# Keys of three units loaded as 32x32 blocks: VectorE's transposes behind the last item of a unit, stores on ScalarE's queue

## The chip, the cores and the metric

The kernel runs on one core of one Trainium2 chip. Times are device microseconds (us) of whole executions; a profile shows one execution. The engines are named as in the profile: PE is TensorE (matrix products), PEld its weight loads, DVE is VectorE, ACT ScalarE, POOL GpSimd, SP SyncE, which here only issues transfers; "ACTq" and "SPq" are transfers issued by ACT and SP. Every run told here was in the fast state.

## The reference, cut to what matters

A retention block (a causal linear attention with a decay per head) feeds a multiplicative feed-forward network, all in float32.

```python
# q, k, v: (8 batches, 8 heads, 576 positions, 64)
scores = q @ k.T / 8
ret    = scores * gamma[h] ** (i - j)   # for i >= j, else 0
x      = (ret @ v)  as (8*576, 512)
a, b   = x @ w1, x @ w2                 # (512, 1024) each
out    = ((a * b) @ w3) @ w_out         # (1024, 1024), (1024, 512)
```

## The kernel before

The attention works in *units*: a pair of batches (four pairs) and one of five chunks of positions (one of 64 and four of 128), so units 0 to 19. A unit needs q and k transposed (`qT`, `kT`), scores `sc`, their product with the mask `pm`, the output products `xps`, and a running state `st`. Between the units stand *items* of the feed-forward part: `up` (seven products, 9.1 us of PE) and `down` (seven products, 12.1 us of PE, followed by stores of 128 rows twice). From the second pair on, the feed-forward part of one pair fills the gaps of the next pair's attention.

The transposes come in two kinds. `front` transposes on PE and copies from PSUM with ScalarE. `front_blocks` needs an operand that was loaded as 32x32 blocks, placed so that VectorE's transposes within the blocks give the whole transpose; such a load is 16 small transfers of 32 KB for a unit of 128 positions.

```python
def load_blocks(g, nm):                       # 16 issues for 128 positions
    t = pools["ld"].tile([P, 2 * NP, P // BL, BL], F32, tag="ld_q", name="bl_" + nm)   # two buffers
    for a in range(2):
        for f in range(D // BL):
            for m in range(n):
                nc.sync.dma_start(t[part:part + BL, :, m, :], ...)
def front_blocks(g, names="kq"):
    for nm in names:
        dst = pools["fr"].tile(..., tag=nm + "T", bufs=1 if nm == "k" else 2)
        nc.vector.transpose(dst[...], live["bl_" + nm, g][...])
# ... cut ...
in_blocks = [u > 2 * NC for u in range(G)] + [False] * 2     # NC = 5: k by blocks from unit 11 on
for g in range(NC, G):
    n = -(-len(todo) // (NC - c))                            # items of this unit
    if g + 2 < G and not in_blocks[g + 2]:
        load(g + 2, "k"); load_blocks(g + 2, "q")
    if g + 1 < G:
        scale(g + 1, "v")                                    # GpSimd
        if not in_blocks[g + 1]:
            front(g + 1, "k")                                # PE transposes
            front_blocks(g + 1, "q")                         # VectorE transposes
    half = (n + 1) // 2
    if in_blocks[g + 1]:
        scale_blocks(g + 1)                                  # GpSimd scales q's blocks
        work(1)
        front_blocks(g + 1)
        half = max(half - 1, 0)
    if in_blocks[g + 2]:
        load_blocks(g + 2, "q"); load_blocks(g + 2, "k")
    work(half)
    pv(g)                                                    # output products
    # ... loads of v (and k) of unit g + 2, then:
    state(g + 1); score(g + 1)
    work(n // 2)
```

`aside` is a list of VectorE operations; each addition inside an `up` item takes one from it, and a `down` item empties it before its last addition. In `down` the output buffer `ot` exists once, so its first copy must wait for the stores of the item before.

Of the kernel before, what the change touches and what calls it, by code (L numbers as in the profile page):

```python
# [40 lines left out]
def kernel(  # L41
# [13 lines left out]
    nc = tc.nc  # L55
# [13 lines left out]
    NC = (S + P - 1) // P  # L69
# [3 lines left out]
    G = NB2 * NC  # L73
    NB = 3
# [5 lines left out]
    NQ = DF // QC  # L80
# [26 lines left out]
    def load(g, names, engine=nc.sync):  # L107
        i, c = divmod(g, NC)
        sz = sizes[c]
        src = {"k": k, "q": q, "v": v}  # L110
        for nm in names:
            t = pools["ld"].tile([P, 2 * H, D], F32, tag="ld_" + nm, name="ld_" + nm)
            engine.dma_start(
                t[:sz], src[nm][2 * i:2 * i + 2, :, starts[c]:starts[c] + sz, :].rearrange("b h p d -> p (b h) d"))
            live[nm, g] = t
# [27 lines left out]
    for c in (0, slice(1, NC)):  # L143
        n = short if c == 0 else P
# [34 lines left out]
    def load_blocks(g, nm):  # L179

        i, c = divmod(g, NC)
        n = sizes[c] // BL
        t = pools["ld"].tile([P, 2 * NP, P // BL, BL], F32, tag="ld_q", name="bl_" + nm)
        src = {"k": k, "q": q}[nm][2 * i:2 * i + 2].rearrange("b (p a) s d -> a (b p) s d", a=2)
        for a in range(2):
            for f in range(D // BL):
                part = (a * (D // BL) + f) * BL
                for m in range(n):
                    s0 = starts[c] + m * BL
                    nc.sync.dma_start(t[part:part + BL, :, m, :],  # L190
                                      src[a, :, s0:s0 + BL, f * BL:(f + 1) * BL].rearrange("m r x -> r m x"))
        live["bl_" + nm, g] = t

    def scale_blocks(g):
        c = g % NC
        n, n0 = sizes[c] // BL, starts[c] // BL
        t = live["bl_q", g]
        for b in range(2):
            part = t[:, b * NP:(b + 1) * NP, :n, :]
            nc.gpsimd.tensor_tensor(  # L200
                out=part, in0=part, in1=gqs[:, :, n0:n0 + n].unsqueeze(3).to_broadcast([P, NP, n, BL]),
                op=ALU.mult)

    def front_blocks(g, names="kq"):
        c = g % NC
        n = sizes[c] // BL
        for nm in names:
            dst = pools["fr"].tile([P, 2, NP, P], F32, tag=nm + "T", name=nm + "T", bufs=1 if nm == "k" else 2)
            nc.vector.transpose(
                dst[:, :, :, :sizes[c]].rearrange("p b m (n x) -> p (b m) n x", x=BL),  # L210
                live["bl_" + nm, g][:, :, :n, :])
            live[nm + "T", g] = dst

    def scale(g, nm, scalar=False):
        c = g % NC
        sz = sizes[c]
        t, gam = live[nm, g], {"q": gq, "v": gk}[nm]
        t = t[:sz].rearrange("p (b h) d -> p b h d", b=2)
        if scalar:
            for h in range(H):  # L220
                nc.scalar.mul(t[:, :, h, :], t[:, :, h, :], gam[:sz, c, h:h + 1])
            return
        nc.gpsimd.tensor_tensor(  # L223
            out=t, in0=t, in1=gam[:sz, c].unsqueeze(1).unsqueeze(3).to_broadcast([sz, 2, H, D]), op=ALU.mult)

    def front(g, names="kq"):
        c = g % NC
        sz = sizes[c]
        for nm in names:
            src = live[nm, g]  # L230
            dst = pools["fr"].tile([P, 2, NP, P], F32, tag=nm + "T", name=nm + "T",
                                   bufs=1 if nm == "k" and g >= NC else 2)
            for b in range(2):
                tp = acc.tile([P, NP, P], F32, tag="acc", name="tp")
                for p in range(NP):
                    h = b * H + 2 * p
                    nc.tensor.transpose(tp[:, p, :sz],  # L237
                                        src[:sz, h:h + 2, :].rearrange("p a d -> p (a d)"),
                                        ident[:sz, :sz])
                nc.scalar.copy(dst[:, b, :, :sz], tp[:, :, :sz])  # L240
            live[nm + "T", g] = dst

    def score(g):
        c = g % NC
        sz = sizes[c]
        kT, qT = live["kT", g], live["qT", g]
        pm = pools["fr"].tile([P, 2, 2, NP, P], F32, tag="pm", name="pm", bufs=1)
        for b in range(2):
            sc = [acc.tile([P, NP, P], F32, tag="acc", name="sc") for j in range(2)]
            for p in range(NP):  # L250
                for j, hs in enumerate(heads):
                    nc.tensor.matmul(sc[j][:sz, p, :sz], kT[hs, b, p, :sz], qT[hs, b, p, :sz],  # L252
                                     start=True, stop=True)
            for j in range(2):
                nc.vector.tensor_mul(pm[:sz, b, j, :, :sz], sc[j][:sz, :, :sz],  # L255
                                     mask[:sz, :sz].unsqueeze(1).to_broadcast([sz, NP, sz]))
        live["pm", g] = pm
# [284 lines left out]
    aside = []  # L542
# [53 lines left out]
    def ahead(x, y, n=3):  # L596
        todo_sums = pair_of(x, y)[2]
        for _ in range(min(n, len(todo_sums))):
            aside.append(todo_sums.pop(0))
# [60 lines left out]
    stores, keep_stores = [], []  # L660

    def store():
        while stores:
            nc.sync.dma_start(*stores.pop(0))


    load_block()
# [85 lines left out]
    todo = [(0, 1, 2), (0, 0, 3), (0, 1, 3)] + [(0, 2, fp) for fp in range(NQ - 1)]  # L753
# [34 lines left out]
    todo = [(down, (0, 0), (0, 1)), (down, (1, 0), (1, 1)), (down, (0, 2), (1, 2))]  # L788

    def add_pair(i):  # L790

        for n in range(NB):
            m = every.index((i, n))
            if m != NB:
                todo.append((up, i, n, 1))
            if m > NB and m % 2 == 0:
                todo.append((down, (m - 2, 2), (m - 1, 2)))
            todo.extend((up, i, n, fp) for fp in range(2, NQ))
            if m + 1 < len(every):
                todo.append((up, *every[m + 1], 0))  # L800
                if m % 2 == 0:
                    todo.append((carry, m, 2))
            else:
                todo.append((down, (m - 1, 2), (m, 2)))
            todo.append((down, (m, 0), (m, 1)))

    def work(n):
        for _ in range(min(n, len(todo))):
            fn, *args = todo.pop(0)

            nxt = next((x for x in todo if x[0] is not carry), None)
            if nxt and nxt[0] is down and fn is not carry:
                if fn is down:
                    args.append(nxt[1:])
                else:
                    last = args == [*every[max(nxt[1][0], nxt[2][0])], NQ - 1]
                    ahead(*nxt[1:], 1 if last else 3)
            if g == G and not todo:
                fn(*args, last=True)
            else:  # L820
                fn(*args)

    g = NC
# [3 lines left out]
    state(NC)  # L827
    score(NC)
    scale_blocks(NC + 1)
    in_blocks = [u > 2 * NC for u in range(G)] + [False] * 2  # L830
    for g in range(NC, G):
        c = g % NC
        n = -(-len(todo) // (NC - c))
        if g + 2 < G and not in_blocks[g + 2]:
            load(g + 2, "k")
            load_blocks(g + 2, "q")
        if g + 1 < G:
            scale(g + 1, "v")
            if not in_blocks[g + 1]:
                front(g + 1, "k")  # L840
                front_blocks(g + 1, "q")
        half = (n + 1) // 2
        if in_blocks[g + 1]:
            scale_blocks(g + 1)
            work(1)
            front_blocks(g + 1)
            half = max(half - 1, 0)
        if in_blocks[g + 2]:
            load_blocks(g + 2, "q")
            load_blocks(g + 2, "k")  # L850
        work(half)
        pv(g)

        if g + 2 < G:
            queue = nc.scalar if in_blocks[g + 2] else nc.sync
            load(g + 2, "v", queue)
            if in_blocks[g + 2] and (g + 2) % NC != NC - 1:
                load(g + 2, "k", queue)
        if g + 1 < G:
            state(g + 1)  # L860
            score(g + 1)
        if g + 2 < G and not in_blocks[g + 2]:
            scale_blocks(g + 2)
        if g == NC + 1:
            strassen_tokens(1, 0)
            todo.extend((up, 1, 0, fp) for fp in range(2))
        work(n // 2)
        if c == NC - 1:
            add_pair(g // NC)
    g = G  # L870
# [44 lines left out]
```

## Time and profile before

| | before |
|---|---|
| median of three runs | 863.84 us (861.37 to 864.35) |
| span of the profiled run | 858.3 us |
| PE busy | 846.7 us |
| VectorE, ScalarE, GpSimd busy | 475.0, 182.2, 115.9 us |
| PE idle between 225 and 840 us | 0.22 us |

A busy PE is read together with its waits. An engine that is busy all the time and waits for nothing sets the time by the sum of its instructions. The prediction below shows the lines.

### The profile page before, as it was taken

What the parts mean: (1) busy time and instruction counts of PE and PEld (TensorE: products, weight loads), DVE (VectorE), ACT (ScalarE), POOL (GpSimd) and SP (SyncE); (2) the same over time, 40 slices, a digit from 0 to 9 for tenths busy, and PEclk for the clock granted to TensorE, in tenths of its full rate; (3) what the DMA queues carried; (4) which work ended last, traced back from release to release, by engine and by line L of the source; (5) the groups of instructions that cost most, each with busy time, mean ns of one, the idle gap of its engine ahead of it and who ended that gap; (6) DMA issues with size and microseconds to landing.
All of it is one profiled execution on the core that took longest, in us unless ns stands there. A gap on an engine that the chain in (4) does not pass through costs nothing.

```text
span 858.3 us, 15385 instructions
## 1 busy us (share of the span) xinstructions
PE 846.7 (99%) x6317; PEld 773.3 (90%) x6317; DVE 475.0 (55%) x794; ACT 182.2 (21%) x364; POOL 115.9 (14%) x96
## 2 busy tenths in 40 slices
PE   9999999999999999999999999999999999999998
PEld 8889999544998999999999999999999999999996
DVE  4899998995754344553544443535543334335343
ACT  3766333342122111101101101111101101001000
POOL 3000020001214214203023120230400101000000
PEclk9999999999999999999999999999999999999999
DMA  9994453455247524415231525061200000000001
GB/s 197 228 213 115 100 100 99 123 147 81 33 105 142 97 49 83 80 42 107 53 70 28 89 45 115 19 106 25 51 25 26 2 25 1 26 25 1 25 1 49
DMA packets 205062, 63.21 MB, mean 74 GB/s; under 512 B 186936, under 2 KB 195384, under 8 KB 204992
## 3 DMA queue, kind: packets, MB, share of 16 engines
q1 hardware_dynamic: 172352, 54.07, 30.5%
q10 hardware_dynamic: 32640, 8.16, 5.0%
q8 instruction: 49, 0.80, 0.4%
q14 instruction: 21, 0.17, 0.1%
HBM read 52.76 MB, written 9.44 MB: 72 GB/s over the span
## 4 chain that ended last, share of the span: by engine, by line
PE 88%; DVE 3%; SPq 1%; issue 1%; DMA 1%; ACT 0%; DVEq 0%; ACTq 0%
PE up L506 46%; PE po L617 25%; PE ps L461 6%; PE sc L252 4%; PE xps L309 3%; PE xps L302 2%; PE st L274 1%; PE tp L237 1%; SPq L746 1%; DVE c L511 1%; DMA raw<-in_moe_w_out_dram 0%; DVE e L400 0%; SPq L349 0%; DVE w L411 0%; DMA out_dram<-ot 0%
## 5 line engine op out<-in xcount | busy, mean ns | idle before, releaser
L511 DVE TENSOR_TENSOR c<-up,c 128x384 f32<-128x384 f32 x240 | 133.2, 555 | 183.8 <-PE up L506 179.1
L506 PE MATMUL up<-xT,wA 128*128 128x192 f32 x1152 | 212.0, 327 | 0.6 <-ACT c L519 0.6
L506 PEld LDWEIGHTS up<-xT,wA 128*128 128x128 f32 x1152 | 190.6, 190 | 3.1 <-ACT c L519 0.9
L506 PE MATMUL up<-T,wS 128*128 128x192 f32 x768 | 140.5, 326 | 0.0
L506 PEld LDWEIGHTS up<-T,wS 128*128 128x128 f32 x768 | 127.4, 190 | 0.0
L617 PE MATMUL po<-w3o,ab 128*128 128x256 f32 x456 | 104.2, 380 | 0.3 <-ACT ot L639 0.3
L617 PEld LDWEIGHTS po<-w3o,ab 128*128 128x128 f32 x456 | 85.9, 190 | 12.3 <-ACT ot L639 0.7
L621 DVE TENSOR_TENSOR ot<-po,ot 128x256 f32<-128x256 f32 x90 | 38.2, 424 | 74.4 <-PE po L617 71.6
L506 PE MATMUL up<-xT,wS 128*128 128x192 f32 x384 | 70.6, 327 | 0.6 <-DVE c L511 0.5
L531 ACT COPY c<-up 128x384 f32<-128x384 f32 x48 | 22.9, 478 | 225.5 <-PE up L506 221.3
L255 DVE TENSOR_TENSOR pm<-sc,mask 128x512 f32<-128x512 f32 (+1 forms) x80 | 45.5, 629 | 45.1 <-PE sc L252 45.1
L506 PE MATMUL up<-T,wA 128*128 128x192 f32 x384 | 70.3, 326 | 0.0
L617 PE MATMUL po<-wB,forms 128*128 128x256 f32 x288 | 65.3, 379 | 0.0
L506 PEld LDWEIGHTS up<-xT,wS 128*128 128x128 f32 x384 | 63.5, 190 | 1.5 <-DVE c L511 1.5
L506 PEld LDWEIGHTS up<-T,wA 128*128 128x128 f32 x384 | 63.7, 190 | 0.0
L617 PEld LDWEIGHTS po<-wB,forms 128*128 128x128 f32 x288 | 54.6, 190 | 7.7 <-issue 0.3
L223 POOL TENSOR_TENSOR ld_v<-ld_v,gk 128x1024 f32<-128x1024 f32 (+1 forms) x17 | 32.8, 1928 | 198.7 <-DMA ld_v<-in_v_dram 160.7
L461 PE MATMUL ps<-wo,w3T 128*128 128x512 f32 x128 | 55.4, 593 | 1.3 <-DVE w3T L415 1.3
L461 PEld LDWEIGHTS ps<-wo,w3T 128*128 128x128 f32 x128 | 23.9, 190 | 32.1 <-issue 30.5
L480 POOL TENSOR_TENSOR T<-xT,T 128x384 f32<-128x384 f32 x20 | 20.9, 1044 | 214.0 <-PE up L506 212.4
L537 DVE TENSOR_TENSOR ab<-c 128x768 f32<-128x768 f32 x48 | 47.0, 980 | 3.8
L519 ACT COPY c<-up 128x384 f32<-128x384 f32 x48 | 22.9, 477 | 118.8 <-PE up L506 70.1
(77 smaller groups left out, 817.2 us busy)
## 6 DMA issues: line engine op xcount, KB each, us to landing
raw<-in_moe_w_dram SPq DMA_DIRECT2D x64, 128.0 KB, 3.0
bl_q<-in_q_dram SPq DMA_DIRECT2D x208, 32.0 KB, 2.2
out_dram<-ot SPq DMA_DIRECT2D x23, 256.0 KB, 2.0
bl_k<-in_k_dram SPq DMA_DIRECT2D x136, 32.0 KB, 2.3
raw<-in_moe_w_dram SPq DMA_DIRECT2D x8, 512.0 KB, 7.5
raw<-in_moe_w_dram SPq DMA_DIRECT2D x16, 256.0 KB, 6.7
ld_k<-in_k_dram SPq DMA_DIRECT2D x8, 512.0 KB, 7.8
ld_v<-in_v_dram SPq DMA_DIRECT2D x8, 512.0 KB, 7.4
```

What stands on the lines that cost most here:

```text
L223: nc.gpsimd.tensor_tensor(out=t, in0=t, in1=gam[:sz, c].unsqueeze(1).unsqueeze(3).to_broadcast([sz, 2, H, D]), op=ALU.mult)
L252: nc.tensor.matmul(sc[j][:sz, p, :sz], kT[hs, b, p, :sz], qT[hs, b, p, :sz], start=True, stop=True)
L255: nc.vector.tensor_mul(pm[:sz, b, j, :, :sz], sc[j][:sz, :, :sz], mask[:sz, :sz].unsqueeze(1).to_broadcast([sz, NP, sz]))
L309: nc.tensor.matmul(banks[r][heads[half], b, n, :sz], vs[:sz, b * H + 2 * p + j, :], pm[:sz, b, j, p, :sz], start=(c == 0 and m == 0), stop ...
L461: nc.tensor.matmul(ps, live["w3T", ft][:, g, :], live["wo"][:, g, :], start=(g == 0), stop=(g == KF - 1))
L506: nc.tensor.matmul(ps[:, w, :], a[:, w, r, :], b[:, r, :], start=(new and w == r == 0), stop=(w == r == 1), skip_group_check=True)
L511: nc.vector.tensor_add(c[:, to], ps, c[:, sb])
L519: nc.scalar.copy(c[:, 0], p1)
L531: nc.scalar.copy(c[:, 0], p1)
L537: nc.vector.tensor_mul(ab[:, 4 * fp:4 * fp + 4, :], c[:, :, 0, :], c[:, :, 1, :])
L617: nc.tensor.matmul(ps[nm], a[A][:, f, :], live["W"][B][:, f, :], start=(f == 0 and not on), stop=(f == NP - 1), skip_group_check=True)
L621: nc.vector.tensor_add(ot[:, to[0], to[1]], ps[nm], ot[:, sb[0], sb[1]])
```

## The change

Its intent is to take PE's transposes of k out of three more units: 8 and 9 (the second pair's last two) and 10 (the third pair's short one). To make room, items move between units 7 to 9, VectorE's transposes go behind all items of a unit, and stores go out on ScalarE's queue. Cut to its core:

```diff
     def store():
         while stores:
-            nc.sync.dma_start(*stores.pop(0))
+            nc.scalar.dma_start(*stores.pop(0))
...
-            todo.extend((up, i, n, fp) for fp in range(2, NQ))
+            if m != NB:
+                todo.extend((up, i, n, fp) for fp in range(2, NQ))
...
-    in_blocks = [u > 2 * NC for u in range(G)] + [False] * 2
+    in_blocks = [u >= 2 * NC - 2 for u in range(G)] + [False] * 2
...
-        n = -(-len(todo) // (NC - c))
+        n = (1, 1, 1, 3, 1)[c] if g < 2 * NC else -(-len(todo) // (NC - c))
...
             scale_blocks(g + 1)
+            work(n - 1)
+            aside.extend(lambda nm=nm: front_blocks(g + 1, nm) for nm in "kq")
             work(1)
-            front_blocks(g + 1)
-            half = max(half - 1, 0)
+            while aside:
+                aside.pop(0)()
+            half = 0
...
-            todo.extend((up, 1, 0, fp) for fp in range(2))
-        work(n // 2)
+            todo.extend((up, 1, 0, fp) for fp in range(NQ))
+        if not (in_blocks[g + 1] and g + 1 < G):
+            work(n // 2)
```

## The prediction

> **What bounds the kernel now.** I read the page's busy shares first, then the stretches by window, the waits of TensorE, and the chain of waits in order of time around the units that the change touches.
>
> ```profile
> span 858.3 us, 15385 instructions
> PE 846.7 (99%) x6317; PEld 773.3 (90%) x6317; DVE 475.0 (55%) x794; ACT 182.2 (21%) x364; POOL 115.9 (14%) x96
> ```
>
> TensorE (PE) is busy 846.7 of 858.3 us, so all its idle time is 11.6 us. VectorE has 45% of the span free, ScalarE 79%. The windows (span, then busy time of each engine, clock, DMA share, GB/s) show where those 11.6 us lie:
>
> ```profile
> 225.00:320.00 95.00, 95.00 (x931) 85.88 (x930) 46.78 (x73) 18.41 (x41) 24.37 (x19) 1.00 0.45 88
> 320.00:400.00 80.00, 80.00 (x692) 75.75 (x688) 38.50 (x61) 10.26 (x22) 16.61 (x13) 1.00 0.43 77
> 550.00:560.00 10.00, 9.78 (x150) 8.97 (x149) 6.40 (x9) 3.08 (x5) 0.00 (x0) 1.00 0.43 81
> 848.00:858.30 10.30, 6.97 (x33) 5.80 (x31) 2.81 (x6) 0.37 (x1) 0.00 (x0) 0.94 0.19 52
> ```
>
> From 225 us to 840 us only one window has any PE idle, 0.22 us at 550 to 560. The rest of the 11.6 us is in the first 225 us (about 7.8 us by the same windows), which the change does not touch, and in the last 18 us (0.28 + 3.33). The waits of PE after 200 us say the same; columns are the total, times, longest:
>
> ```profile
> PE po L617 <- ACT ot L639: 0.3, 1, 0.3
> PE sc L252 <- DVE qT L209: 0.2, 1, 0.2
> ```
>
> So in the changed region the span is the sum of what PE executes, and waits of the other engines cost nothing. The chain there, with start, length and instructions:
>
> ```profile
> 273.26 1.99 PE sc L252 x32
> 275.25 1.02 PE tp L237 x8
> 276.27 12.09 PE po L617 x56
> ...
> 292.22 1.99 PE sc L252 x32
> 294.21 1.02 PE tp L237 x8
> 295.23 9.10 PE up L506 x56
> ...
> 307.26 1.99 PE sc L252 x32
> 309.25 0.48 PE tp L237 x8
> 309.73 9.30 PE up L506 x56
> ```
>
> The three "tp" pieces are the PE transposes of k for units 8, 9 and 10 (the second pair's last two units and the third pair's 64-token unit), each squeezed between a unit's scores and the next item. These are what the change removes.
>
> **What the Trainium skill says.** "VectorE: DVE Perf Modes", section "The three transpose paths": VectorE's transpose works in 32x32 blocks only and writes SBUF, TensorE does a whole 128x128 and writes PSUM. The kernel agrees: VectorE's STREAM_TRANSPOSE of kT takes 1.24 us (median) for 128x1024 and needs operands loaded by blocks; the PE route is 8 transposes and two ScalarE copies from PSUM (586 ns each, median). "TensorE: Matmul & The Clock Gate", section "Part 4: PE-mode transpose", gives about 275 ns for one transpose in a kernel; the trace's median is 272 ns, but they are pipelined, and eight occupy PE for 1.02 us, 128 ns each. That is the number that counts. "Perfetto Trace Analysis", section "Identifying the Most-Contended Engine", warns that matmul busy time is no measure of headroom and points to weight-load time: PEld is 90%, so the reading "PE bound" stands. "DMA: Bandwidth & Descriptors", section "Issuing engines are not separate DMA queues": moving an issue to another engine saves only the issuing sequencer's time. Here a store's issue is 0.33 to 0.60 us on SyncE, and nothing on PE's path waits for SyncE.
>
> **The change part by part.**
>
> 1. *PE transposes removed.* With no transpose between them, the next item follows scores directly. Elsewhere in the chain a down item after scores takes 12.28 us (at 428.27) and after a transpose 12.09, an up item 9.30 against 9.10. Unit 8 saves 1.02 - (12.28 - 12.09) = 0.83. Unit 9 saves 1.02 - (9.30 - 9.10) = 0.82. At unit 10 the up item takes 9.30 already behind the short transpose, so all 0.48 is saved. Sum 2.13 us, all on the path. Six PSUM copies on ScalarE go too; that is off the path.
>
> 2. *VectorE transposes of k added.* Two of 1.24 us and one of about 0.71 us (the minimum of kT), 3.2 us on an engine that is idle half of the time: nothing on the path if they end in time (rivals below).
>
> 3. *Block loads of k for units 8 to 10 (16 + 16 + 8 issues of 32 KB)*, at about 0.5 us each on SyncE, 20 us there. The loads of v, and of natural k for units 8 and 10, go to ScalarE's queue. Hidden where an item of 9 to 12 us or more lies between buffer and use.
>
> 4. *Transposes behind all items of a unit.* Both are put between the accumulations of the last item. One up item has five VectorE additions (0.56 us) and one product (0.96) in 9.1 us of PE, 3.8 us of work; two transposes make 6.2, and three sums for a following down item at about 0.7 to 0.9 make at most 8.7. The hard date is the addition that frees the PSUM tile which the seventh product continues in: by my count it ends about 6.95 us after the item's start and is needed at 7.9 us. So 0.95 us of slack, and no stall, provided that the block data are there. This order should remove the 0.22 us wait of scores for qT, which comes at a carry item with the transposes right behind it; none of the new unit ends falls on a carry by my count.
>
> 5. *Stores on ScalarE's queue.* 49 issues at 0.47 us median make 23 us of ScalarE's sequencer; ScalarE is 21% busy. It now stands in order behind VectorE's last addition of a down item, which ends about 0.4 us after PE, or some 2 us later when two transposes lie before it. ScalarE's next duty is at least 1.4 us after (first copy of an up item), and PE needs that copy only several us later. No effect on PE. The last store still leaves behind the last addition: end unchanged within 0.1 or 0.2 us.
>
> 6. *Unit counts (1, 1, 1, 3, 1).* The same up and down items, in another order; PE work unchanged.
>
> **Rivals.**
>
> A. *Unit 10 comes too late.* Its only filler item is one up item, so it has the shortest notice. v of unit 10 can be loaded only when the output products of unit 8 have read its buffer, and GpSimd scales v before it scales q's blocks. In the kernel before:
>
> ```profile
> 307.34 0.64 SPq L113 DMA_DIRECT2D ld_v<-in_v_dram  x1
> 311.56 1.90 POOL L223 TENSOR_TENSOR ld_v<-ld_v,gk 64x1024 f32<-64x1024 f32 x1 [10.67 <-DMA ld_v<-in_v_dram]
> ```
>
> Counted from the end of those products: the issue now comes behind four ScalarE copies (1.2 us), landing 4.2 to 6.3 us later (the shortest median and the SyncE median of this transfer), v scaled 1.9 us later, q's blocks 1.2 us later, so 8.5 to 10.6. The transpose of 0.7 and an addition of 0.56 bring 9.8 to 11.9. The item starts at 2.06 (after scores) and its seventh product wants to start 7.9 later, at 9.97. So the stall is 0 to 1.9 us, and I count 0.5. In its full size it eats most of part 1: about 863.5.
>
> B. *Stores block ScalarE.* An in-order wait for a store, or slow issues behind the loads of k on the same queue (one took 2.39 us), delays the copies that free PSUM. For it: 23 us of issues and waits for VectorE that ScalarE did not have. Against it: ScalarE waits for PE 221 us in one group alone, so its copies come early, and seven PSUM banks cover a delay of a few us. If each of some 18 down items cost 0.2 us, the gain would be gone: 865 to 867.
>
> C. *A hidden gain from freeing SyncE.* Its waits for the last additions are long:
>
> ```profile
> SPq L664 <- DVE ot L621: 272.5, 29, 46.3
> ```
>
> Loads behind such a store start late. But PE waits for no load after 200 us, so the gain has an upper bound of 0.5 us (the two waits shown). Even everything together gives 2.13 + 0.5 = 2.6 us, or 861.2.
>
> **Range and chances.** 863.84 - 2.13 (transposes) - 0.22 (wait at a carry) + 0.5 (unit 10) = 862.0. The three runs before span 861.37 to 864.35, and their median lies near the top, so a fresh median could lie half a us lower: I say 861.6. One us of scatter on either side and rivals A and B above give 859.3 to 864.2. Two per cent is 17 us; PE can't be relieved of that (it has 11.6 us of idle time in all), and a loss of that size would need a new wait of about 1 us at nearly every down item. So within 2% is 0.98.
>
> **What would show it.** Right: 24 fewer "tp" pieces of PE, their time down by about 2.5 us; PE idle from 225 to 840 us under 1.5 us; kT by STREAM_TRANSPOSE twelve times instead of nine; the span 1 to 3 us shorter. Rival A would show as TensorE waiting for a VectorE addition in an up item just before unit 10, with VectorE itself waiting for GpSimd's scaled q. Rival B would show as TensorE waiting for ScalarE's copies of c, ot or xT after 235 us. I am wrong if the span moves by more than 3 us either way: that would mean that PE's own pace changed, or that a wait repeats at each unit.

## The result, and the profile after

The changed kernel took 859.18 us (median of four runs, 858.59 to 859.42) against 863.07 us (four runs, 861.37 to 864.35). The ratio is 0.9955, 95% interval 0.9935 to 0.9975. Ratios are the mean time of one kernel's fast runs over that of the other's of the same rounds, so not quite the ratio of the medians. The time is within 2% of before, as predicted, but 0.12 us under the predicted range of 859.3 to 864.2, and the gain of 3.9 us is larger than the sum of all parts allowed (2.6 us). So the first question is where the rest came from.

The page's first lines for the changed kernel:

```profile
span 857.7 us, 15368 instructions
PE 844.7 (98%) x6293; PEld 770.5 (90%) x6293; DVE 482.6 (56%) x797; ACT 179.1 (21%) x358; POOL 119.7 (14%) x96
```

There are 24 PE instructions less and 2.0 us less PE time. But the two profiled spans differ by only 0.6 us. The same window as before (span, then PE, weight loads, VectorE, ScalarE, GpSimd busy), and PE's waits after 200 us:

```profile
225.00:320.00 95.00, 94.63 (x825) 86.28 (x824) 49.17 (x75) 14.62 (x32) 22.21 (x16) 1.00 0.42 79
```

```profile
PE sc L252 <- ACT qT L240: 0.4, 1, 0.4
PE po L617 <- ACT ot L639: 0.3, 1, 0.3
```

The wait of scores for VectorE's qT is gone. A wait for ScalarE's qT has come. The chain at units 8 and 10 (start, length, what):

```profile
274.95 1.99 PE sc L252 x32
276.93 12.28 PE po L617 x56
...
325.49 1.99 PE sc L252 x32
327.48 9.30 PE up L506 x56
```

No transposes stand between scores and items, and the items take just the 12.28 and 9.30 us that the prediction took from other places of the old chain. The tile kT shows who does the work now (count, then shortest, median and longest ns; it was x9 before):

```profile
L209 DVE STREAM_TRANSPOSE kT<-bl_k x12: 702/1234/1245, 287.9 to 657.8; 128x1024 f32<-128x1024 f32 x10, 128x512 f32<-128x512 f32 x2
```

Unit 10, for which the prediction feared most, in the timeline (start, length, engine; in brackets the idle time before and what ended it):

```profile
330.56 1.90 POOL L223 TENSOR_TENSOR ld_v<-ld_v,gk 64x1024 f32<-64x1024 f32 x1 [27.19 <-DMA ld_v<-in_v_dram]
...
333.65 0.71 DVE L209 STREAM_TRANSPOSE qT<-bl_q 128x512 f32<-128x512 f32 x1 [0.73 <-POOL bl_q L200]
...
335.31 1.46 PE L506 MATMUL up<-xT,wS 128*128 128x192 f32 x8
```

Unit 8's output products ended at 325.49. GpSimd began v 5.1 us later and VectorE could transpose q 8.2 us after them; the count had said 8.5 to 10.6 until then. VectorE did stand 0.73 us, but the addition needed ended at about 334.84 (the pair of additions from 334.28 on takes 0.56 each) and PE's seventh product began on time at 335.31. Rival A cost nothing, by half a microsecond.

And the wait for ScalarE's qT at 239 us:

```profile
235.75 2.80 ACTq L665 DMA_DIRECT2D out_dram<-ot  x3
...
238.59 0.65 ACT L240 COPY kT<-tp 128x256 f32<-128x256 f32 x2 [4.89 <-DMA out_dram<-ot]
...
239.56 1.15 PE L252 MATMUL sc<-qT,kT 64*64 64x64 f32 x32 [0.37 <-ACT qT L240]
```

The first down item keeps its stores back until the next loads are issued. On ScalarE's queue these stores now stand ahead of the copies of unit 5's transposes, and the last of them waits for VectorE's last addition (which ended at 238.09). PE's scores came 0.37 us late.

### The profile page after: what moved, and what is told of

Read it like the earlier page. It is cut to its first block, busy times and chain, and to the rows that moved or that the text cites. A ratio compares the mean times of both kernels' runs of the same rounds, so it can differ in the third digit from the quotient of the medians.

```text
span 857.7 us, 15368 instructions
## 1 busy us (share of the span) xinstructions
PE 844.7 (98%) x6293; PEld 770.5 (90%) x6293; DVE 482.6 (56%) x797; ACT 179.1 (21%) x358; POOL 119.7 (14%) x96
## 4 chain that ended last, share of the span: by engine, by line
PE 88%; DVE 4%; issue 1%; ACT 1%; DMA 0%; ACTq 0%; DVEq 0%
PE up L506 46%; PE po L617 25%; PE ps L461 6%; PE xps L309 4%; PE sc L252 4%; PE xps L302 2%; PE st L274 1%; DVE c L511 1%; PE tp L237 1%; DMA out_dram<-ot 0%; DVE e L400 0%; ACT e L389 0%; DVE w L411 0%; DVE ab L537 0%; DVE wS L169 0%
```

## The experiments

Twelve kernels ran in three jobs, each job on another chip; all gave right results. "Before" in a line is the kernel before in the same rounds: 35, 27 and 53 runs in the three jobs, with medians of 861.38, 861.82 and 861.81 us.

### 1. Both kernels again, and each with the other's store queue

The two repeats are unchanged copies. The other two each change one line:

```diff
# stores_only: the kernel before
-            nc.sync.dma_start(*stores.pop(0))
+            nc.scalar.dma_start(*stores.pop(0))
# after_stores_on_sync: the changed kernel
-            nc.scalar.dma_start(*stores.pop(0))
+            nc.sync.dma_start(*stores.pop(0))
```

Expected of the copy of before:

> An unchanged copy of the kernel before, to see its scatter. The two profiles differ by only 0.6 us in span, and from 225 us on by 1.85 us, while the medians differ by 3.9 us. Theory S (start): the change is worth about 2 us, and the rest of the 3.9 us is scatter of the load-bound first 225 us in few runs of before: then this copy's median lies within 1.5 us of 861.5 in many runs, its slow runs being slow before 225 us. Theory Q (queue): the kernel before has a wait in its slower runs that its profiled run happened not to show, from 225 us on, and the change removes it: then this copy repeats about 863 us and the changed kernel about 859.

Measured: 861.81 us median of 13 runs (859.71 to 863.29), ratio 0.9997 (0.9985 to 1.0009).

Expected of the copy of the changed kernel:

> An unchanged copy of the changed kernel. Theory S: 1.5 to 2.5 us faster than the kernel before in these rounds (ratio 0.997 to 0.998). Theory Q: 3.5 to 4.5 us faster (ratio 0.995 to 0.996), with less scatter than the kernel before.

Measured: 860.00 us median of 10 runs (859.02 to 861.17), ratio 0.9974 (0.9963 to 0.9985). So the change is worth about 0.26%, 2.2 us (1.3 to 3.2 by the interval; the medians of this job, 861.38 and 860.00, are 1.4 apart), as theory S said, and not 3.9. The kernel before takes about 861.8 us: its 119 runs in all have a median of 861.75, with a tenth at 860.02 or below and a tenth at 863.84 or above. The three runs that the prediction started from, with their median of 863.84, were a slow sample, and the four runs of the changed kernel in the result were a somewhat fast one.

**Where the scatter comes from.** In the twelve profiles whose code is the same up to there, the first down item begins anywhere from 223.06 to 227.76 us: up to 4.7 us of difference before the first instruction that the change touches. A second, smaller piece comes just behind that point. In the profile of before_again:

```profile
227.19 2.61 POOL L223 TENSOR_TENSOR ld_v<-ld_v,gk 128x1024 f32<-128x1024 f32 x1
228.07 2.27 DVE L587 TENSOR_TENSOR forms<-ab 128x512 f32<-128x512 f32 x1
```

VectorE's sum takes 0.69 us where it stands alone in the same item; here, beside GpSimd's scaling, it takes 2.27, and PE waits 0.4 us for it. In half of the profiles it takes 1.42 and PE does not wait; the next sum is slow instead. In both cases the slow sum ends 0.54 or 0.55 us after GpSimd's instruction (229.80 and 230.34 here). (The Trainium skill, "SBUF — State Buffer", section "Who interferes with whom", says that a VectorE instruction with two SBUF inputs contends with a GpSimd instruction that reads SBUF. The trace agrees.) So the two profiles are best compared from the first down item to the end, and only where that sum has the same length. With 1.42 us: before 858.3 - 223.47 = 634.83, changed 857.7 - 224.56 = 633.14, a gain of 1.69. With 2.27 us: before_again 860.1 - 224.56 = 635.54, after_again 858.3 - 224.04 = 634.26, a gain of 1.28. In after_again PE waited another 0.4 us for the sum before that one (L583, which took 1.53 us beside GpSimd and 1.08 in before_again); without this wait the second pair gives the same 1.7 as the first.

Expected of the stores alone:

> The kernel before with its stores on ScalarE's queue and nothing else. Theory S: no gain; slower by about 0.4 us, the wait of the first scores for ScalarE's copies behind the kept stores (ratio 1.000 to 1.001). Theory Q with stores on SyncE as the cause: about 2 us faster (ratio 0.997 to 0.998).

Measured: 861.85 us, ratio 1.0004 (0.9994 to 1.0013), and the wait of 0.4 us at the first scores is in its profile. The store queue by itself gains nothing. With this, and with before_again at 861.81 and not at 863, theory Q falls.

Expected of the changed kernel with its stores back on SyncE:

> The changed kernel with its stores back on SyncE's queue. Theory S: as the changed kernel or 0.4 us faster, as long as the block loads behind the stores still come in time (ratio to before 0.9965 to 0.998). Theory Q: about 2 us slower than the changed kernel, and a wait of TensorE after 225 us that is not there with the stores on ScalarE.

Measured: 865.34 us (863.66 to 868.24, nine runs), ratio 1.004 (1.0026 to 1.0054): 5.3 us slower than the changed kernel. Neither theory had that size. Its timeline:

```profile
267.41 14.01 SPq L190 DMA_DIRECT2D bl_k<-in_k_dram  x16
...
281.52 2.67 SPq L665 DMA_DIRECT2D out_dram<-ot  x3
...
286.39 3.78 PE L617 MATMUL po<-w3o,ab 128*128 128x256 f32 x8 [4.50 <-ACT ot L639]
```

The stores of a down item stand behind the 32 block issues of unit 8. Their data was ready at 273.5 us, but they were issued from 281.5 on. The next down item's first copy needs the buffer `ot` free, so PE waited 4.50 us. Then its first eight instructions took 3.78 us, where they take 1.99 in an undisturbed run (at 846.07 in the kernel before): PE ran at about half pace behind the wait. The move of the stores is therefore no gain of its own; it is what makes the block loads affordable.

### 2. One part of the change undone or moved

**kept_stores_sync** sends only the kept stores of the first down item by SyncE again:

```diff
-    def store():
+    def store(queue=nc.scalar):
         while stores:
-            nc.scalar.dma_start(*stores.pop(0))
+            queue.dma_start(*stores.pop(0))
...
-    store()
+    store(nc.sync)
```

> The changed kernel, but the stores kept from the first down item go out on SyncE's queue as before; all later stores stay on ScalarE's. Theory W (the kept stores block ScalarE): TensorE's wait of 0.4 us for ScalarE's copy of qT at about 239 us vanishes and the time falls by 0.4 us (ratio to before 0.9965 to 0.9972 against 0.9974). Rival: the wait is only moved to another place (same ratio).

Measured: 859.49 us (22 runs, 857.53 to 862.1), ratio 0.9974 (0.9963 to 0.9984). In the profile the wait is gone, PE is busy in every window from 225 to 840 us, and from the first down item to the end it takes 855.9 - 223.42 = 632.48 us. That is 2.35 less than before, where the prediction had 2.13 + 0.22; with one profile of each kernel, the agreement to the hundredth is partly luck. From the first down item to the next one the chain takes 16.42 us before, 16.41 here and 17.01 in the changed kernel. So the kept stores cost 0.60 us, more than the 0.37 us that PE stood idle, and without them the changed kernel's gain of 1.69 would be 2.29. Timed, this is below what the rounds resolve, and the changed kernel was timed in another job, so the ratio doesn't decide.

**transposes_after_first_item** puts VectorE's transposes where they were:

```diff
             scale_blocks(g + 1)
-            work(n - 1)
-            aside.extend(lambda nm=nm: front_blocks(g + 1, nm) for nm in "kq")
             work(1)
-            while aside:
-                aside.pop(0)()
-            half = 0
+            front_blocks(g + 1)
+            half = max(half - 1, 0)
...
-        if not (in_blocks[g + 1] and g + 1 < G):
-            work(n // 2)
+        work(n // 2)
```

> The changed kernel with VectorE's transposes behind the first item of a unit and the rest of the items split around the output products, as before the change; counts, blocks and queues stay. Theory P (my prediction's part 4: placement is off the path): 0 to 0.5 us slower than the changed kernel (ratio 0.9974 to 0.9980), the 0.2 us wait of scores for qT may come back. Rival L: with the transposes earlier, unit 9's block loads (32 issues of half a us, 16 us, begun when unit 8's transposes free the buffers) come too late, VectorE stands before the transpose with additions behind it, and TensorE waits 2 us or more.

Measured: 871.51 us (four runs), ratio 1.0121 (1.0104 to 1.0138). Rival L holds, and by more than it said. Its timeline at unit 9:

```profile
311.11 1.25 DVE L209 STREAM_TRANSPOSE kT<-bl_k 128x1024 f32<-128x1024 f32 x1 [5.37 <-DMA bl_k<-in_k_dram]
...
315.30 2.82 PE L506 MATMUL up<-xT,wS 128*128 128x192 f32 x8 [3.42 <-DVE c L511]
```

The block loads could begin at 290.62, when unit 8's transposes freed the buffers, and k's last block was there at 311: 20.5 us, where rival L had counted 16 us for the issues. The 32 issues took 0.58 us each (9.79 + 8.85 us), not 0.5. VectorE stood for 5.37 us with additions behind it, PE waited 3.42 us, and the product behind the wait took 2.82 instead of 1.46 us. The same happens once more at 370 us (4.2 us of wait).

**blocks_and_queue_only** is the kernel before with two lines of the change:

```diff
-            nc.sync.dma_start(*stores.pop(0))
+            nc.scalar.dma_start(*stores.pop(0))
-    in_blocks = [u > 2 * NC for u in range(G)] + [False] * 2
+    in_blocks = [u >= 2 * NC - 2 for u in range(G)] + [False] * 2
```

> The kernel before with units 8 to 10 by blocks and the stores on ScalarE's queue; the order of items, their counts and the place of the transposes as before. By my count unit 9's transposes wait for the block loads until about 15 us after unit 8's scores began, so its scores come 3 us late: time 0 to 3 us above the kernel before (ratio 1.000 to 1.004), with a wait of TensorE's scores for VectorE's qT of 2 to 4 us. Rival: the loads are in time and the gain is there without the new order (ratio 0.997 to 0.998).

Measured: 880.82 us (five runs), ratio 1.0222 (1.0202 to 1.0242), the only one that is slower by over 2%:

```profile
315.36 1.25 DVE L209 STREAM_TRANSPOSE kT<-bl_k 128x1024 f32<-128x1024 f32 x1 [7.14 <-DMA ld_k<-in_k_dram]
...
317.88 3.79 PE L252 MATMUL sc<-qT,kT 64*128 64x128 f32 x32 [8.39 <-DVE qT L209]
```

The profile puts VectorE's wait down to a load of plain k, which this instruction does not read; which load held it is not shown. The wait of scores for qT is 8.4 us instead of the 2 to 4 expected, and there is another of 6.0 us in an up item at 360 us. Scores behind the wait took 3.79 us instead of 2.06. So taking the transposes off PE, without the new order, costs 19 us instead of gaining 2.

**blocks_from_unit7** goes one unit further, on top of kept_stores_sync:

```diff
-    in_blocks = [u >= 2 * NC - 2 for u in range(G)] + [False] * 2
+    in_blocks = [u >= NC + 2 for u in range(G)] + [False] * 2
```

> A further step: the changed kernel with the kept stores on SyncE and unit 7 by blocks too. Eight more PE transposes go, worth 0.83 us by the same sum as for unit 8. Theory T (PE time is all that counts): 1.2 us faster than the changed kernel (ratio to before 0.9958 to 0.9966). Rival: unit 7's block loads start at 243 us, when unit 6's transpose frees the buffer, and are used at about 269 us; if they or GpSimd's scaling are late, a wait of TensorE for VectorE takes the gain (ratio 0.9974 or more).

Measured: 865.83 us (six runs), ratio 1.0052 (1.0038 to 1.0066). Unit 7 was in time. It was unit 8 that came late: its loads begin only when unit 7's transposes free the buffers (273.7 us), k is complete at 298.0 us, 24.3 us later, and only one down item stands between; scores waited 4.6 us.

This profile also shows where some of the scatter at the start comes from. The first line is from this run, the second the same instructions in kept_stores_sync:

```profile
49.91 1.97 PE L237 MATMUL tp<-ident,ld_q 128*128 128x128 f32 x8 [2.84 <-POOL ld_q L223]
```

```profile
48.43 1.09 PE L237 MATMUL tp<-ident,ld_q 128*128 128x128 f32 x8 [2.14 <-POOL ld_q L223]
```

After a wait of 2.84 us the transposes take 1.97 us instead of 1.09, and the 64 products that follow are slow too. The window over them (0.58, the value behind the busy times of the five engines, is the granted clock):

```profile
50.00:57.00 7.00, 7.00 (x88) 6.34 (x90) 6.09 (x12) 5.09 (x13) 0.00 (x0) 0.58 1.07 227
```

The clock that PE was granted was 0.58 there and 1.00 in the windows after. The Trainium skill, "TensorE: Matmul & The Clock Gate", section "Part 1: The HAM clock gate", says that PE falls to half its clock after an idle window of about 3.4 us. The waits of 3.42, 4.50 and 8.39 us above agree: the granted clock behind them was 0.53, 0.50 and 0.50. The wait of 2.84 us is shorter, but 1.09 us of transposes stand before it, and the same page's Part 4 says that transposes do not count as busy; the sum is 3.9 us. This sum is no rule, though. In after_stores_on_sync a wait of 2.11 us at the same place, 3.2 with the transposes, was enough (granted clock 0.50 from 50 to 52 us):

```profile
48.81 1.97 PE L237 MATMUL tp<-ident,ld_q 128*128 128x128 f32 x8 [2.11 <-POOL ld_q L223]
```

In before_again 2.25 us, 3.3 with the transposes, was not (clock 1.00). What decides is open. What goes with it can be read, from a comparison and not from an experiment. In the fourteen profiles the clock from 50 to 52 us was 0.50 to 0.58 five times and 1.00 nine times. From the start of these transposes to the first down item the five took 176.51 to 177.85 us and the nine 174.98 to 175.94. The transposes themselves began anywhere from 47.73 to 49.91. So the scatter at the start has two parts of like size: when this point is reached, up to 2.2 us, and whether half pace follows, 0.6 to 2.9 us.

### 3. How much notice the blocks need, and the scatter

**counts_11122** takes one up item away from between unit 8's and unit 9's transposes:

```diff
-        n = (1, 1, 1, 3, 1)[c] if g < 2 * NC else -(-len(todo) // (NC - c))
+        n = (1, 1, 1, 2, 2)[c] if g < 2 * NC else -(-len(todo) // (NC - c))
```

> The changed kernel with counts 1, 1, 1, 2, 2: one up item less stands between unit 8's and unit 9's transposes. Theory N: unit 9's notice falls to about 18 us, VectorE stands about 4 us before unit 9's transpose, TensorE waits 2 to 4 us for a VectorE addition[...]: 3 to 8 us slower than the changed kernel (ratio to before 1.001 to 1.007). Rival A of my prediction, that unit 10 is the short one: no slower, or faster (ratio 0.9970 or less).

Measured: 860.85 us (22 runs), ratio 0.9992 (0.9982 to 1.0003).

```profile
308.57 1.25 DVE L209 STREAM_TRANSPOSE kT<-bl_k 128x1024 f32<-128x1024 f32 x1 [2.46 <-DMA bl_k<-in_k_dram]
...
311.90 1.57 PE L506 MATMUL up<-xT,wS 128*128 128x192 f32 x8 [1.25 <-DVE c L511]
```

Theory N has the direction and not the size: VectorE stood 2.46 us, PE waited 1.25 us for it, the slow stretch that theory N counted on behind the wait did not come (the product took 1.57 us), and most of the gain is gone. Rival A is refused: giving unit 10 more time brought nothing, as PE did not wait there in the changed kernel either.

**unit7_counts_11221** gives units 8 and 9 two items each on top of blocks_from_unit7:

```diff
-        n = (1, 1, 1, 3, 1)[c] if g < 2 * NC else -(-len(todo) // (NC - c))
+        n = (1, 1, 2, 2, 1)[c] if g < 2 * NC else -(-len(todo) // (NC - c))
```

> Blocks from unit 7 on, kept stores on SyncE, and item counts 1, 1, 2, 2, 1 instead of 1, 1, 1, 3, 1, so that units 8 and 9 each have two items between the release of the block buffers and their transposes. Theory N (notice: 32 block issues plus scaling need 22 to 25 us from release to transpose, as the last runs showed, and TensorE keeps a slack of 1 us beyond): both gaps are about 24 us, so the wait of 4.6 us is gone or under 1.5 us, and eight PE transposes less than in the changed kernel are worth 0.83 us and the kept stores 0.4: ratio to before 0.9958 to 0.9975. Rival: the two gaps are both a little short and cost over 2 us each: ratio 1.000 or more.

Measured: 859.52 us (16 runs), ratio 0.9975 (0.9964 to 0.9987). PE's wait of 4.6 us is gone. From the first down item to the end it takes 856.9 - 224.85 = 632.05 us, 0.43 less than kept_stores_sync instead of 0.83. The rest is lost at unit 8:

```profile
292.62 1.25 DVE L209 STREAM_TRANSPOSE kT<-bl_k 128x1024 f32<-128x1024 f32 x1 [1.28 <-DMA bl_k<-in_k_dram]
...
294.41 1.46 PE L506 MATMUL up<-xT,wA 128*128 128x192 f32 x8
...
295.95 1.57 PE L506 MATMUL up<-xT,wS 128*128 128x192 f32 x8
```

VectorE stood 1.28 us for k's blocks, its additions came late, and PE's last product began 1.54 us after the one before, not 1.30, and took 1.57 us, not 1.46: 0.35 us in all. In time the version can't be told from the changed kernel.

**changed_keep_busy** gives PE six idle products (twelve PE instructions) in the wait at 46 us:

```diff
     scale(3, "v", True)
+    keep_busy(6)
     front(3, "q")
```

> The changed kernel with six idle matmuls for TensorE at about 46 us, in the wait for GpSimd's scaled q of unit 3, about 1.5 us in a wait of 2.1 us. Theory H (part of the scatter of all these kernels is that this wait sometimes is long enough for TensorE to fall to half pace): the slow tail goes; of some ten or more runs none lies over 861.5, the median is unchanged or up to 0.5 us lower. Rival: the scatter comes from the arrival of loads before that; then the runs spread as before (1.5 us or more below and above the median).

Measured: 860.08 us (22 runs, 858.13 to 862.90), ratio 0.9979 (0.9969 to 0.9989). Two of the 22 runs lie above 861.5, and the spread is no smaller, so what theory H forecast did not come. But the edit does not decide about the theory, because it hardly shortened the wait: the idle products ran at once, from 46.27 to 47.77 us, and left 1.71 us of waiting.

**unit7_keep_busy** has both of the last two edits:

> The version with unit 7 by blocks, counts 1, 1, 2, 2, 1, kept stores on SyncE, and the six idle matmuls. If theories N and H both hold it is the fastest: 1 to 1.8 us below the changed kernel (ratio to before 0.9953 to 0.9965). If N fails it is as slow as the run without the idle matmuls.

Measured: 859.26 us (six runs, 857.94 to 860.09), ratio 0.9964 (0.9949 to 0.9978). In its profile half pace came in spite of the idle products (granted clock 0.58 from 50 to 52 us):

```profile
49.70 1.40 PE L237 MATMUL tp<-ident,ld_q 128*128 128x128 f32 x8 [1.92 <-POOL ld_q L223]
```

Its median is the lowest of all the experiments, but the interval covers the changed kernel's 0.9974. I found no version that clearly beats the changed kernel.

## Why the prediction was right or wrong

- **The transposes (part 1): right.** The items behind scores take 12.28 and 9.30 us as counted. Where nothing else interferes (kept_stores_sync), the part of the span that the change touches is 2.35 us shorter, the predicted 2.13 + 0.22.
- **VectorE's additional work and unit 10 (parts 2 and 4, rival A): right for the changed kernel, and by less than I thought.** PE never waited for it. But calling the placement harmless was only half of it: I gave a slack of 0.95 us and did not ask what the old placement would cost. It costs about 12 us (871.51 against 860.00, in another job). PE's slack at unit 10 was half a us, and the 0.5 us of stall that I counted there did not come. (A sum in part 4 is wrong: 6.2 and three sums of up to 0.9 make 8.9, not 8.7.)
- **Block loads (part 3): the size was off.** "About 0.5 us each" measured 0.58 in a burst of 32, and the whole chain from free buffers to a transposable k 20.5 to 24.3 us, where rival L had 16 for the issues. The changed kernel gives unit 9 27.5 us (289.17 to 316.64), which is why it holds.
- **Stores (part 5, rival B): wrong twice.** "No effect on PE" fails at the kept stores: PE waited 0.37 us for ScalarE's qT, and the chain grew by 0.60. And the statement that nothing on PE's path waits for SyncE was true of the kernel before only: with 32 more issues ahead of the stores it is false, and leaving the stores there costs 5.3 us.
- **The bound on the gain (rival C): right.** 2.6 us at most; 2.2 us measured (ratio 0.9974), 1.7 between like profiles.
- **The step that failed is the base.** "Their median lies near the top, so a fresh median could lie half a us lower": it lay 2.1 us lower (863.84 against 861.75 in 119 runs). I took a median of three for the time of the kernel before, although its own profiled run, at 860.07, was below all three. The first 225 us scatter by up to 4.7 us for the same code. With 861.75 the same sum of parts gives 861.75 - 1.85 = 859.9, and the repeat measured 860.00. Luck has a share in this: 0.5 us for unit 10 was counted and not paid, 0.6 us for the kept stores was paid and not counted, and the two nearly cancel. The repeat lies inside the predicted range; the first four runs (859.18) were a fast sample as well.
- **The signs named beforehand.** The 24 pieces fewer, kT twelve times and PE idle under 1.5 us (0.37) came. The profiled span fell by 0.6 us, not by 1 to 3, and the first medians moved by 3.9, more than the 3 that were to mean another pace of PE or a wait at each unit. The profiles show neither from 225 us on; what is left for both numbers is the scatter of the start.

What stays open is why the start is reached early or late, and why half pace follows the wait at 46 us in some executions only. The mean granted clock of a run does not tell: of the 115 runs of before in the experiments, the 25 with 0.992 or less took 863.09 us on average and the 27 with 0.999 or 1.0 took 860.95, but counts_11122 and after_again, with 0.992 in their profiles, had half pace from 9 to 21 us and still began the first down item at 223.06 and 224.04, two of the four earliest. Runs without a profile show no stages, so that their scatter lies in the start is inferred from the profiles.

## What to carry to other kernels

When one engine is busy all the time, count what leaves it and bound the gain by its idle time; that sum was right to a few tenths. But take the base from many runs or from the profile, because a true gain of 2 us is smaller than the scatter of a start that waits for loads. And when work moves from the busy engine to one that has time, the price is notice: find when the buffers come free, add issues, landing and scaling, and set enough items in between (here k's last block was there 20.5 to 24.3 us after the buffers came free), with nothing urgent queued behind the issues.

## What the Trainium skill lacked or had wrong

- "DMA: Bandwidth & Descriptors", section "Issuing engines are not separate DMA queues", says that the issuing time saved by another engine is usually small beside the transfer. Here a burst of 32 issues took 18.6 us while one landed in 2.2 us, and a store behind such a burst left 8 us late; putting stores on the other queue was worth 5.3 us.
- "TensorE: Matmul & The Clock Gate", section "Part 1: The HAM clock gate", has the half clock after an idle window of about 3.4 us. Here waits of 1.92, 2.11, 2.12, 2.20 and 2.84 us before the transposes at about 49 us were followed by a granted clock of 0.50 to 0.58, and waits of 2.12 to 2.25 at the same place in other executions by 1.00. The length of a wait near 2 us did not tell which would come.
- "VectorE: DVE Perf Modes", section "The three transpose paths", has times for bf16 only, and no page has a measured one for float32. In float32, VectorE took 1.24 us for 128x1024, and eight transposes of TensorE in a row 1.02 us.
